# Moving the filter's second transform ahead of the first pair's ticks, with grouped turning transfers and another order at the borders

## The chip, the cores and the metric

The kernel runs on one core of one Trainium2 chip. The metric is device time in microseconds of a whole launch; lower is better. Engines are called PE (TensorE), DVE (VectorE), ACT (ScalarE), POOL (GpSimd) and SP (SyncE); PE writes to PSUM, eight banks of 512 f32 per partition, and DVE and ACT empty PSUM into SBUF.

## What is computed

A causal long convolution along the sequence, by FFT, and a spectral mixing layer behind it. Sizes: batch 8, sequence 5696, width 128, 64 modes.

```python
Xf = rfft(x, n=2*S, axis=1);  Hf = rfft(h, n=2*S, axis=0)      # x: (8, 5696, 128), h: (5696, 128)
x = irfft(Xf * Hf[None], n=2*S, axis=1)[:, :S, :]
X = rfft(x, axis=1)                                            # 64 modes are mixed
Yr = einsum('bmd,mde->bme', Xr, w_r) - einsum('bmd,mde->bme', Xi, w_i)
Yi = einsum('bmd,mde->bme', Xr, w_i) + einsum('bmd,mde->bme', Xi, w_r)
u = x + irfft(Y, n=S, axis=1)
out = u + maximum(u @ w_ch, 0)
```

## The kernel before

The sequence of 5696 is 89 rows of 64, and a transform of length 2 × 5696 is done in two steps. The **first transform** multiplies by F (the tile F1, 90 frequencies as 180 real columns). It is `a_tile(j)` for the input: 32 tiles of 4 matmuls with 180 columns each, into two PSUM banks, emptied by ACT or DVE into As (128x720). The **second transform** multiplies by the matrix M (`second`), four of the 90 frequencies at a time; such a group is a **tick**, and there are NT = 23 (the last has two frequencies). The input is worked in four pairs of batches (`g_` = 0 to 3).

In tick t of a pair PE and the other engines do four things, staggered so that they overlap: `second` (As and M into PSUM), `products` (ACT copies PSUM to Xs, DVE multiplies Xs by the filter Hs into U; L600), then with a lag of LC = 2 ticks the **third step** (U times Wc, 4 matmuls with 512 columns, cast by ACT into Zs or Zt, and written to the DRAM scratch zscr by SP), and with a lag of LM = 3 ticks the **modes** (Zs times G, added up in bank 7 over the whole pair, copied to XT at the end). `x_load` and `x_place` bring the next pair's input during the ticks, on POOL's DMA queue and on DVE.

The filter h goes through the same two transforms once. Its first transform (into Ah) is done ahead of everything while the input x arrives. Its second is `filter_tick(t)`: 16 small matmuls of Ah with M, one evacuation to Hs (128x512), and two DMAs on SP's queue that write a **turned copy**, the upper and the lower 64 partitions exchanged, into the second half of Hs (46 transfers in all); after every second tick up to the 11th a piece of G is loaded over the used part of Ah. Six filter ticks stand among the first pair's 32 tiles. The other 17 stand in the first pair's own ticks, six ticks ahead (LH), in banks 2 and 3 with DVE as the evacuating engine.

The first pair's ticks therefore have an order of their own: one `second` per tick, in banks 0 and 1 as long as the filter uses 2 and 3, all products from Xs, six buffers of Zs at first. In the other pairs two seconds are issued together every other tick (`twin`), in two alternating pairs of banks, and every fourth product is read from PSUM directly (`straight`).

The **border** between two pairs is written out by hand in the table `border`: a_tiles 0 to 5 of the next pair are put at given places in ticks 22 to 25, where the third steps and modes of the last ticks are still to be done; tiles 6 to 31 follow, ACT and DVE taking turns in a fixed pattern. `share(n)` is the other way to choose the engine: it keeps a running total for ACT and DVE by assumed costs (670 and 815 ns for 720 columns, 480 and 600 for 512) and gives the work to the one that is done earlier. `keep(n, bank)` issues n filler matmuls that keep PE going while it waits.

After the fourth pair come the mixing of the modes and the stage that makes the output (`u_z`, `u_tile`, `o_tile`).

All instructions go through a recorder that derives the waits from the tokens that each instruction reads and writes; each engine runs its own list in the order of issue.

Of the kernel before, what the change touches and what calls it, by code (L numbers as in the profile page):

```python
# [123 lines left out]
def bass_long_conv_fft__then__afno_spectral_mix_kernel(nc, x, h, moe_w_r, moe_w_i, moe_w_ch, out):  # L124
    B, S, D = x.shape
    M = moe_w_r.shape[0]
    assert D == P and M == 64 and B == 8
    J = 64
# [4 lines left out]
    NP = B // 2  # L133
    KT = 4
# [94 lines left out]
    NU, NXS, NZ, NZX = 3, 2, 6, 10  # L229
    NZS = [NZ] + [NZX] * (NP - 2) + [8]  # L230
    NZL = NZS[-1]
# [222 lines left out]

    def filter_tick(t, banks, eng="vector"):
# [84 lines left out]

    LC, LM, LH = 2, 3, 6
    ZR = 96
    XBANKS = [bank(0), bank(1), bank(2), bank(3)]

    def with_h_at(g_, t):
        return g_ == 0 and t + LH < NT

# [55 lines left out]
    Z_OLD = [("ag", k) for k in range(NS, NS + 8 * (NZX - NZ))]  # L603
    XPLACE = [9, 10, 12, 15, 16, 18, 20, 22], [9, 10, 13, 14, 17, 18, 20, 22]

    def zroom(g_, s_):
        return (s_ - 2 * NZ) % NZX if g_ == 0 and s_ >= 2 * NZ else s_ % NZS[g_]

    def xtok(n):
        return [("xt", n, p_) for p_ in range(2)]  # L610

    def tick(g_, t):
        if g_ + 1 < NP:
            for i in range(2 * XC):
                if t == XPLACE[g_ > 0][i]:
                    x_place(i, x_st[i], xtok(i))
        with_h = with_h_at(g_, t)
        if t < NT:
            of_two = t > 0 and twin(g_, t - 1)
            if not of_two and not (g_ == 0 and t > LC):  # L620
                second(g_, t)
            products(g_, t, slot_of(g_, t))
            if twin(g_, t):
                second(g_, t + 1)
                if straight(g_, t):
                    copied(g_, t + 1, slot_of(g_, t + 1))
        drain = list(border[t]) if t in border and g_ + 1 < NP else []
        if drain and t >= NT:
            j, sl, e = drain.pop(0)
            a_tile(j, [sl], e)  # L630
        if g_ + 1 < NP and t % 2 == 0 and 0 < t <= 4 * XC:
            i = t // 2 - 1
            x_load(g_ + 1, i, x_st[i], xtok(i), [("u", t % NU)] + AST)
        if LC <= t < NT + LC:
            s_ = t - LC
            n = len(ticks[s_])
            i, zi = s_ % NU, zroom(g_, s_)
            zb = [turns("z", ZBANK) for b in range(2)]
            for b in range(2):
# [9 lines left out]
                [("zs", zi, 0), ("zs", zi, 1)], [("zd", g_, s_)])  # L649
            if drain and t >= NT:  # L650
                j, sl, e = drain.pop(0)
                a_tile(j, [sl], e)
        if g_ == 0 and LC <= t < NT - 1:
            second(g_, t + 1)
        if LM <= t < NT + LM:
            s_ = t - LM
            zi = zroom(g_, s_)
            for b in range(2):
                for i, k in sorted(enumerate(ticks[s_]), key=lambda q: (s_ > 0 or q[1] != 1, q)):
                    if k % 2:  # L660
                        o, off, n, sl = pv(MB, b * P, [[1, P]]), (k + 1) // 2 * P, P, (k + 1) // 2
                    else:
# [5 lines left out]
                       k == 1 and b == 0, k == NK - 1 and b == 1, [("g", sl // GP), ("zs", zi, b)], [bank(MB)])  # L668
        if drain and t < NT + LM - 1:
            j, sl, e = drain.pop(0)  # L670
            a_tile(j, [sl], e)
        if with_h:
            filter_tick(t + LH, [2, 3])

    SLOTS = [0, 2, 4, 6]
    for j in range(32):
        a_tile(j, [turns("s", SLOTS)], "both" if j == 31 else share(720))
        if j >= 11 and j % 3 == 2 and (j - 11) // 3 < LH:
            b_ = turns("s", SLOTS)
            filter_tick((j - 11) // 3, [b_, b_ + 1], share(512))  # L680
    keep(12, turns("s", SLOTS))
    for g_ in range(NP):
        for t in range(NT + LM):
            tick(g_, t)
            if g_ == 0 and t < 2:
                keep(8, 4)
            assert g_ + 1 < NP or not wp
            if g_ == NP - 1 and t in early:
                pace[:] = [("u", min(t, NT - 1) % NU)]
                early[t]()  # L690
        evac(bass.AP(xt, 2 * g_ * XTW + M, [[B * XTW, P], [XTW, 2], [1, P]]), pv(MB, 0, [[P, 2], [1, P]]),
             [bank(MB)], [("xt", g_)], 1.0 / 64, eng="scalar", after=[("ag", k) for k in range(NS + 2 * XN, NK)])
# [199 lines left out]
```

## Time and profile before

| | us |
|---|---|
| median of 3 runs | 386.07 (385.49 to 386.13) |
| the profiled execution | 385.34 |
| its span, first to last instruction | 383.2 |
| PE busy | 366.0 (96%) |
| DVE busy | 310.5 (81%) |
| ACT busy | 302.7 (79%) |
| POOL busy | 82.5 (22%) |

A line of the profile names the source line, the engine, the operation, and output and input tiles by the program's names without buffer numbers; "x16" is a count. All matmuls are recorded by one helper (L320), so they are told apart by tiles: F,Xin is the first transform of the input, Ah,M the filter's second transform, As,M the input's second, U,Wc the third step, G with Zs or Zt the modes, and F alone is filler. ACT's As is L310, DVE's As L314; DVE's Hs is the filter's evacuation (L312). Times in the timeline are microseconds from the start of the span. Matmuls overlap, so the step from one start to the next tells what a group takes. The granted clock of TensorE (PEclk) is 1.00 at full speed.

### The profile page before, as it was taken

The numbers are of one execution on the slowest core, as the hardware profiler recorded it, in microseconds if no ns is written. First come the engines' busy times: TensorE is split into PE (matmuls) and PEld (weight loads), VectorE is DVE, ScalarE is ACT, GpSimd is POOL, SyncE is SP. The second block draws the span as 40 slices with busy tenths as digits, with TensorE's granted clock in tenths as the row PEclk, the third lists the DMA queues.
The fourth block names the chain that finished last, engine by engine and source line by source line (L and its number), as shares of the span: only waits on it lengthen the run. The fifth ranks groups of instructions, "written<-read, shape, count | busy, mean of one in ns | idle before, by whom it ended". The sixth has DMA issues, their size and how long they took to land.

```text
span 383.2 us, 12588 instructions
## 1 busy us (share of the span) xinstructions
PE 366.0 (96%) x5392; PEld 283.7 (74%) x5392; DVE 310.5 (81%) x348; ACT 302.7 (79%) x488; POOL 82.5 (22%) x133
## 2 busy tenths in 40 slices
PE   7999899999989999989999999999999999999994
PEld 7998756666866666866667866668898988887873
DVE  6969888998888999998998888875447767776876
ACT  1359688898889997989997999995457676776785
POOL 8400022220552320733310411319200000000000
PEclk9999999999999999999999999997999999999999
DMA  7998469999699997999995859999999999999879
GB/s 149 194 283 339 138 125 291 273 244 261 96 138 210 226 249 220 101 133 204 263 257 164 87 167 370 334 327 388 402 402 398 414 405 406 412 405 378 359 279 356
DMA packets 86865, 103.94 MB, mean 271 GB/s; under 512 B 22638, under 2 KB 72430, under 8 KB 83330
## 3 DMA queue, kind: packets, MB, share of 16 engines
q1 hardware_dynamic: 62523, 67.73, 50.5%
q0 software_dynamic: 24288, 35.43, 44.1%
q8 instruction: 42, 0.69, 0.7%
q14 instruction: 12, 0.10, 0.1%
HBM read 70.61 MB, written 51.12 MB: 318 GB/s over the span
## 4 chain that ended last, share of the span: by engine, by line
PE 69%; ACT 10%; DMA 9%; DVE 6%; POOL 2%; issue 2%; SPq 0%; DVEq 0%; POOLq 0%
PE ps L320 69%; ACT As L310 6%; DMA Xr<-in_x_dram 4%; DMA ZT0b<-zscr 4%; POOL Xr L317 2%; DVE As L314 2%; DVE U L592 1%; ACT UT L308 1%; ACT R L826 1%; ACT Zt L308 1%; DVE Xin L356 1%; ACT Xs L308 1%; DVE U L600 1%; DVE O L827 1%; DVE UT L312 0%
## 5 line engine op out<-in xcount | busy, mean ns | idle before, releaser
L600 DVE TENSOR_TENSOR U<-Xs,Hs 128x2048 f16<-128x2048 f16 (+1 forms) x73 | 86.7, 1190 | 12.0 <-ACT Xs L308 10.4
L320 PE MATMUL ps<-U,Wc 128*128 128x512 f16 (+1 forms) x368 | 94.0, 376 | 0.0
L308 ACT CAST Xs<-ps 128x1024 f16<-128x1024 f32 (+1 forms) x77 | 75.0, 979 | 9.0 <-PE ps L320 7.4
L308 ACT CAST Zs<-ps 128x512 f16<-128x512 f32 (+1 forms) x134 | 70.6, 596 | 5.9 <-PE ps L320 5.8
L827 DVE TENSOR_TENSOR O<-ps,R 128x512 f32<-128x512 f32 x81 | 52.6, 686 | 20.5 <-ACT R L826 15.2
L826 ACT ACTIVATE R<-ps 128x512 f32<-128x512 f32 x96 | 51.0, 573 | 14.2 <-PE ps L320 13.7
L314 DVE TENSOR_SCALAR As<-ps 128x720 f16<-128x720 f32 (+1 forms) x64 | 53.2, 880 | 5.1 <-PE ps L320 3.4
L320 PE MATMUL ps<-F,Xin 128*128 128x180 f16 x512 | 52.3, 250 | 2.6 <-DVE Xin L356 1.2
L320 PE MATMUL ps<-As,M 64*128 64x128 f16 x1440 | 50.6, 217 | 4.2 <-DVE U L592 3.0
L320 PEld LDWEIGHTS ps<-As,M 64*128 64x128 f16 x1440 | 40.3, 94 | 17.9 <-issue 8.1
L310 ACT ACTIVATE As<-ps 128x720 f16<-128x720 f32 x68 | 48.0, 768 | 6.4 <-PE ps L320 5.6
L320 PE MATMUL ps<-WI,UT 128*128 128x256 f16 x360 | 52.0, 279 | 0.5 <-DVE O L827 0.4
L320 PEld LDWEIGHTS ps<-F,Xin 128*128 128x128 f16 x512 | 44.5, 155 | 9.5 <-DVE As L314 2.6
L320 PEld LDWEIGHTS ps<-U,Wc 128*128 128x128 f16 x368 | 28.7, 97 | 27.6 <-ACT Zs L308 4.4
L317 POOL DMA_DIRECT2D Xt<-in_x_dram x48 | 26.0, 545 | 104.6 <-PE ps L320 100.2
L308 ACT CAST UT<-ps 128x712 f16<-128x712 f32 x40 | 30.0, 752 | 18.8 <-PE ps L320 17.8
L320 PEld LDWEIGHTS ps<-WI,UT 128*128 128x128 f16 x360 | 39.3, 152 | 4.4 <-issue 2.1
L320 PE MATMUL ps<-IBs,C 128*128 128x356 f16 x128 | 40.1, 323 | 0.6
L320 PEld LDWEIGHTS ps<-G,Zs 128*128 128x128 f16 x524 | 27.4, 96 | 11.7
L600 DVE TENSOR_TENSOR U<-ps,Hs 128x2048 f16<-128x2048 f32 x15 | 34.3, 2284 | 0.0
L320 PE MATMUL ps<-G,Zs 128*128 128x128 f16 (+2 forms) x524 | 32.6, 192 | 0.0
L320 PE MATMUL ps<-F 128*128 128x180 f16 x280 | 27.7, 254 | 2.5 <-DMA F<-cF 2.5
(86 smaller groups left out, 506.1 us busy)
## 6 DMA issues: line engine op xcount, KB each, us to landing
out_dram<-O SPq DMA_DIRECT2D x39, 512.0 KB, 11.4
zscr<-Zs SPq DMA_DIRECT2D x64, 256.0 KB, 6.8
Xt<-in_x_dram POOLq DMA_DIRECT2D x24, 320.0 KB, 7.0
zscr<-Zt SPq DMA_DIRECT2D x24, 256.0 KB, 6.6
W<-wscr POOLq DMA_DIRECT2D x4, 1024.0 KB, 8.9
M<-cM POOLq DMA_DIRECT2D x5, 720.0 KB, 20.5
ZT0a<-zscr SPq DMA_DIRECT2D x3, 1024.0 KB, 14.0
Hs<-Hs SPq DMA_DIRECT2D x44, 64.0 KB, 5.8
```

The costliest lines, as they stand in the source:

```text
L308: R.add(e, lambda h_: h_.copy(dst, src), reads, writes, after=after)
L310: R.add(e, lambda h_: h_.activation(dst, src, COPY, scale=scale), reads, writes, after=after)
L314: R.add(e, lambda h_: h_.tensor_scalar_mul(dst, src, scale), reads, writes, after=after)
L317: R.add(eng, lambda h_: h_.dma_start(dst, src), reads, writes, ring=ring, after=after)
L320: R.add("tensor", lambda h_: h_.matmul(o, l, r, start=st, stop=sp), reads, writes)
L356: R.add("vector", lambda e: e.tensor_copy(bass.AP(x_sb, i * XN * XS, [[XW, NQ], [XS, XN], [1, D]]), bass.AP(src, 0, [[XB, NQ], [D, XN], [1 ...
L592: R.add("vector", lambda e, b=b, s_=s_: e.tensor_tensor(bass.AP(u_s[i], b * 512, [[2048, P], [1024, 2], [1, n * D]]), s_, hv, MULT), [tok, ...
L600: R.add("vector", lambda e: e.tensor_tensor(uv, src, hv, MULT), bk + [("h", t, 0), ("h", t, 1, 0), ("h", t, 1, J)], [("u", i)])
L826: R.add("scalar", lambda e: e.activation(rv, src_r, RELU), bk, [("r", i % NR)], after=once(("r", i % NR), G_ALL + XTT + [("y", 0), ("y", 1 ...
L827: R.add("vector", lambda e: e.tensor_tensor(ov, src_u, rv, ADD), bk + [("r", i % NR)], [key + (h_,)], after=once(key, old))
```

## The change

All 23 filter ticks are done among the first pair's 32 tiles, in twos, spread out by `due`; share() chooses the engine for each. The turned copy is written in five groups of ticks (0 to 1, 2 to 5, 6 to 11, 12 to 17, 18 to 22), two transfers each. The first pair's ticks get the order of the other pairs, and the functions that made the difference are gone. The ticks of a pair with a successor end at 22; the third steps and modes that remain are written out with a_tiles 0 to 4 between them, and the engine of each tile at the border is chosen by share().

```diff
-    NZS = [NZ] + [NZX] * (NP - 2) + [8]
+    NZS = [NZX] * (NP - 1) + [8]
...
+    HEND = [1, 5, 11, 17, NT - 1]
...
     def filter_tick(t, banks, eng):
...
-        for p0, p1 in ((0, J), (J, 0)):
-            dma("sync", h_sb[p0:p0 + J, HW + lo:HW + hi], h_sb[p1:p1 + J, lo:hi], "s", [("h", t, 0)], [("h", t, 1, p0)])
+        if t in HEND:
+            g0 = ([-1] + HEND)[HEND.index(t)] + 1
+            lo = KT * g0 * D
+            for p0, p1 in ((0, J), (J, 0)):
+                dma("sync", h_sb[p0:p0 + J, HW + lo:HW + hi], h_sb[p1:p1 + J, lo:hi], "s", [("h", i, 0) for i in range(g0, t + 1)],
+                    [("h", i, 1, p0) for i in range(g0, t + 1)])
...
-    border = {NT - 1: [(0, 0, V)], NT: [(1, 2, V), (2, 0, V)], NT + 1: [(3, 2, A), (4, 0, V)], NT + 2: [(5, 2, V)]}
...
     def twin(g_, t):
-        return g_ > 0 and t % 2 == 1
+        return t % 2 == 1
     def straight(g_, t):
-        return g_ > 0 and t % 4 == 3
+        return t % 4 == 3
     def slot_of(g_, t):
-        if g_ == 0 or t == 0:
-            return XSLOT[(t + 1) % 2 if t and not with_h_at(g_, t) else 0]
+        if t == 0:
+            return XSLOT[0]
         return XSLOT[((t - 1) // 4 + t) % 2]
...
-    XPLACE = [9, 10, 12, 15, 16, 18, 20, 22], [9, 10, 13, 14, 17, 18, 20, 22]
+    XPLACE = [9, 10, 13, 14, 17, 18, 20, 22]
...
+    def tick(g_, t):
...
+        third(g_, t - LC)
+        modes_of(g_, t - LM)
...
     for j in range(32):
         a_tile(j, [turns("s", SLOTS)], "both" if j == 31 else share(720))
-        if j >= 11 and j % 3 == 2 and (j - 11) // 3 < LH:
+        due = NT if j == 30 else max(0, j - 2) * NT // 28 // 2 * 2
+        while done < due:
             b_ = turns("s", SLOTS)
-            filter_tick((j - 11) // 3, [b_, b_ + 1], share(512))
-    keep(12, turns("s", SLOTS))
+            filter_tick(done, [b_, b_ + 1], share(512))
+            done += 1
+    keep(8, turns("s", SLOTS))
     for g_ in range(NP):
-        for t in range(NT + LM):
+        for t in range(NT + LM if g_ + 1 == NP else NT):
             tick(g_, t)
-            if g_ == 0 and t < 2:
-                keep(8, 4)
...
+        if g_ + 1 < NP:
+            load.update(scalar=600.0, vector=0.0)
+            third(g_, NT - 2)
+            a_tile(0, [0], share(720))
+            a_tile(1, [2], share(720))
+            third(g_, NT - 1)
+            load["scalar"] += 560.0
+            a_tile(2, [0], share(720))
+            modes_of(g_, NT - 3)
+            a_tile(3, [4], share(720))
+            modes_of(g_, NT - 2)
+            a_tile(4, [2], share(720))
+            modes_of(g_, NT - 1)
+            load["scalar"] += 700.0
...
-            for j in range(6, 32):
-                a_tile(j, [(4, 6, 0, 2)[(j - 7) % 4] if j > 6 else 0], "both" if j == 31 else (A, V)[(j - 6) % 9 % 2])
+            for j in range(5, 32):
+                a_tile(j, [(0, 4, 6, 2)[(j - 5) % 4]], "both" if j == 31 else share(720))
                 if j == 31:
-                    keep(8, 6)
+                    keep(8, 2)
```

`third` and `modes_of` are the third step and the modes, taken out of `tick` unchanged.

More of the change, by code (lines that the diff above doesn't have):

```diff
@@ L539, in keep @@
             mm(pv(b0 + i % 2, 0, [[1, 2 * NK]]), f1_sb[:, 0:P], f1_sb[:, :], True, True, [("f1",)], [bank(b0 + i % 2)])
-    LC, LM, LH = 2, 3, 6
+    LC, LM = 2, 3
     ZR = 96
     XBANKS = [bank(0), bank(1), bank(2), bank(3)]
-    def with_h_at(g_, t):
-        return g_ == 0 and t + LH < NT
     onchip = {}
@@ L603, in bass_long_conv_fft__then__afno_spectral_mix_kernel, with third @@
     Z_OLD = [("ag", k) for k in range(NS, NS + 8 * (NZX - NZ))]
-    XPLACE = [9, 10, 12, 15, 16, 18, 20, 22], [9, 10, 13, 14, 17, 18, 20, 22]
+    XPLACE = [9, 10, 13, 14, 17, 18, 20, 22]
     def zroom(g_, s_):
-        return (s_ - 2 * NZ) % NZX if g_ == 0 and s_ >= 2 * NZ else s_ % NZS[g_]
+        return s_ % NZS[g_]
     def xtok(n):
         return [("xt", n, p_) for p_ in range(2)]
[L612 to L635, printed above, removed]
+    def third(g_, s_):
+        if 0 <= s_ < NT:
             n = len(ticks[s_])
@@ L649, in tick, with modes_of @@
                 [("zs", zi, 0), ("zs", zi, 1)], [("zd", g_, s_)])
[L650 to L656, printed above, removed]
+    def modes_of(g_, s_):
+        if 0 <= s_ < NT:
             zi = zroom(g_, s_)
@@ L668, in tick @@
                        k == 1 and b == 0, k == NK - 1 and b == 1, [("g", sl // GP), ("zs", zi, b)], [bank(MB)])
[L669 to L673, printed above, removed]
+    def tick(g_, t):
+        if g_ + 1 < NP:
+            for i in range(2 * XC):
+                if t == XPLACE[i]:
+                    x_place(i, x_st[i], xtok(i))
+        if t < NT:
+            of_two = t > 0 and twin(g_, t - 1)
+            if not of_two:
+                second(g_, t)
+            products(g_, t, slot_of(g_, t))
+            if twin(g_, t):
+                second(g_, t + 1)
+                if straight(g_, t):
+                    copied(g_, t + 1, slot_of(g_, t + 1))
+        if g_ + 1 < NP and t % 2 == 0 and 0 < t <= 4 * XC:
+            i = t // 2 - 1
+            x_load(g_ + 1, i, x_st[i], xtok(i), [("u", t % NU)] + AST)
+        third(g_, t - LC)
+        modes_of(g_, t - LM)
     SLOTS = [0, 2, 4, 6]
+    done = 0
     for j in range(32):
         a_tile(j, [turns("s", SLOTS)], "both" if j == 31 else share(720))
-        if j >= 11 and j % 3 == 2 and (j - 11) // 3 < LH:
+        due = NT if j == 30 else max(0, j - 2) * NT // 28 // 2 * 2
+        while done < due:
             b_ = turns("s", SLOTS)
-            filter_tick((j - 11) // 3, [b_, b_ + 1], share(512))
-    keep(12, turns("s", SLOTS))
+            filter_tick(done, [b_, b_ + 1], share(512))
+            done += 1
+    keep(8, turns("s", SLOTS))
     for g_ in range(NP):
-        for t in range(NT + LM):
+        for t in range(NT + LM if g_ + 1 == NP else NT):
             tick(g_, t)
-            if g_ == 0 and t < 2:
-                keep(8, 4)
             assert g_ + 1 < NP or not wp
```

3 lines of the change are left out of this document (2 added, 1 removed).

## The prediction

> **What bounds the kernel now.** I read the page first, for the engine shares and the chain that ended last, and then the table of stages cut at the places where TensorE (PE) goes from one kind of matmul to the next.
>
> ```profile
> span 383.2 us, 12588 instructions
> PE ps L320 69%; ACT As L310 6%; DMA Xr<-in_x_dram 4%; DMA ZT0b<-zscr 4%; POOL Xr L317 2%; DVE As L314 2%; DVE U L592 1%; ACT UT L308 1%; ACT R L826 1%; ACT Zt L308 1%; DVE Xin L356 1%; ACT Xs L308 1%; DVE U L600 1%; DVE O L827 1%; DVE UT L312 0%
> ...
> core 0: us, PE busy (x) PEld busy (x) DVE busy (x) ACT busy (x) POOL busy (x), PEclk, DMA share, GB/s
> 27.97:43.88 15.91, 15.76 (x236) 13.77 (x237) 14.58 (x19) 14.54 (x20) 0.00 (x0) 1.00 0.78 284
> 43.88:93.03 49.15, 48.00 (x884) 29.60 (x885) 41.87 (x49) 42.09 (x65) 8.89 (x16) 1.00 0.94 228
> 93.03:109.12 16.09, 15.34 (x165) 13.11 (x166) 14.61 (x18) 13.80 (x23) 8.51 (x12) 1.00 0.87 126
> 109.12:148.18 39.06, 37.77 (x605) 24.64 (x605) 36.38 (x32) 37.41 (x60) 9.40 (x18) 1.00 1.07 220
> 148.18:164.28 16.10, 15.33 (x164) 13.09 (x165) 14.60 (x18) 13.40 (x23) 7.77 (x11) 1.00 0.89 129
> 164.28:202.97 38.69, 37.47 (x604) 24.61 (x605) 36.38 (x32) 37.05 (x60) 10.52 (x19) 1.00 1.07 221
> ```
>
> The chain runs on PE for 69% of the span. The rows after it are, in order: the first pair's first transform (a_tile) with six filter ticks, the first pair's ticks, a border, the second pair's ticks, a border, the third pair's ticks. Each row gives length, then busy time by engine. Ticks and the stage before them keep PE nearly full: 48.00 of 49.15, 37.77 of 39.06. A border gives PE 15.33 of 16.10 but also DVE 14.60 and ACT 13.40, so it has two limits close together. The first pair's ticks last 49.15 us, the second's 39.06 and the third's 38.69 for the same transforms; the difference is the filter. The timeline of PE shows it inside one tick, first of pair one (with the filter, then late ones without), then of pair two:
>
> ```profile
> 58.59 0.62 PE L320 MATMUL ps<-As,M 64*128 64x128 f16 x16
> 59.14 0.50 PE L320 MATMUL ps<-G,Zs 128*128 128x2 f16 x8
> 59.57 0.41 PE L320 MATMUL ps<-Ah,M 64*128 64x64 f16 x16
> 59.91 1.04 PE L320 MATMUL ps<-U,Wc 128*128 128x512 f16 x4
> 60.88 0.62 PE L320 MATMUL ps<-As,M 64*128 64x128 f16 x16
> ...
> 85.55 0.62 PE L320 MATMUL ps<-As,M 64*128 64x128 f16 x16
> ...
> 87.39 0.62 PE L320 MATMUL ps<-As,M 64*128 64x128 f16 x16
> ...
> 126.59 1.07 PE L320 MATMUL ps<-As,M 64*128 64x128 f16 x32
> ...
> 130.12 1.07 PE L320 MATMUL ps<-As,M 64*128 64x128 f16 x32
> ```
>
> Columns are start and duration; I subtract starts, because the durations overlap. A tick of pair one takes 60.88 − 58.59 = 2.29 us with a filter tick in it and 87.39 − 85.55 = 1.84 without one; in pair two, two ticks take 130.12 − 126.59 = 3.53, or 1.76 each. In both, PE goes straight from one step to the next, so what is taken out of a tick shortens it.
>
> **The first pair's ticks.** The change takes 17 of the 23 filter ticks out of them, with 34 turning DMAs on SP's queue and 17 evacuations on DVE, as well as 16 filler matmuls, and runs them in the order of pairs two and three (twin ticks, every fourth product read from PSUM, ten z buffers). That order is measured: 39.06 and 38.69. I take 38.9, so this stage gives 49.15 − 38.9 = **−10.25 us** (bounds −10.1 and −10.5).
>
> **The first transform's stage.** The 17 ticks (the last has half the columns, so 16.5) land here, on PE as well as on the two engines that empty PSUM.
>
> ```profile
> 27.97 4.83 PE L320 MATMUL ps<-F,Xin 128*128 128x180 f16 x48 [0.48 <-DVE Xin L356]
> 32.73 0.41 PE L320 MATMUL ps<-Ah,M 64*128 64x64 f16 x16
> 33.07 1.16 PE L320 MATMUL ps<-F,Xin 128*128 128x180 f16 x12
> ...
> 40.67 1.97 PE L320 MATMUL ps<-F,Xin 128*128 128x180 f16 x20
> 42.63 1.10 PE L320 MATMUL ps<-F 128*128 128x180 f16 x12
> 43.88 0.62 PE L320 MATMUL ps<-As,M 64*128 64x128 f16 x16
> ...
> L310 ACT ACTIVATE As<-ps 128x720 f16<-128x720 f32 x19 | 14.1, 783 | 3.3 <-PE ps L320 3.1
> L314 DVE TENSOR_SCALAR As<-ps 128x720 f16<-128x720 f32 x12 | 10.5, 904 | 1.3 <-PE ps L320 0.9
> L312 DVE CAST Hs<-ps 128x512 f16<-128x512 f32 x6 | 4.1, 683 | 0.0
> L308 ACT CAST Zs<-ps 128x512 f16<-128x512 f32 x26 | 14.0, 610 | 0.0
> ```
>
> The first 12 tiles take 32.73 − 27.97 = 4.76 us, 0.397 a tile. A filter tick holds PE for 33.07 − 32.73 = 0.34 us. From 32.73 to 42.63 there are 20 tiles and 6 ticks: 9.90 − 20 × 0.397 = 1.96, or 0.33 a tick with whatever waits it causes. So 16.5 × 0.34 = 5.6 us are added.
>
> That price is only right if the evacuations keep up. Busy time over count gives 14.1/19 = 0.74 us a tile on ACT and 10.5/12 = 0.875 on DVE; both together finish a tile every 0.40 us. A filter tick is 0.683 on DVE; ACT has none here, and its nearest row, the cast of the same 128x512 from the second pair's ticks, gives 14.0/26 = 0.54; together one every 0.30. The new stage is 32 tiles and 22.5 ticks: PE 32 × 0.397 + 22.5 × 0.34 = 20.4 us; evacuation 32 × 0.40 + 22.5 × 0.30 = 19.6. PE stays ahead as the limit by 0.8 us, provided that share() divides the work evenly, which it does by a running total. All evacuations of pair one's ticks were on DVE; here ACT takes part, and that is what covers them.
>
> Filler shrinks from 12 matmuls to 8, but the second transform starts at 43.88, 1.25 us after the last tile's matmuls ended, on the last evacuation, so it only covers that wait. I give 0.2 us back: **+5.4 us**. Bounds: +4.6 if the slack in evacuation also removes most of the 1.25 us; +11.1 if each tick costs the full 0.683 on a saturated DVE (16.5 × 0.67). I stay near the lower, because the six ticks already there, all on DVE, cost 0.33.
>
> [...]
>
> **Waits that move.** The later ticks now need the matrix M early. The rows are its last two pieces, the sizes of a turned copy and of a load of G, and what the DMA engines moved (last column, GB/s) while M came in:
>
> ```profile
> L317 POOL DMA_DIRECT2D M<-cM x2: 552/554/555, 12.8 to 13.3; - x2
> DMA to landing us min/median/max: 23.0/24.4/25.7
> ...
> Hs<-Hs SPq DMA_DIRECT2D x44, 64.0 KB, 5.8
> G<-cG SPq DMA_DIRECT2D x5, 256.0 KB, 3.7
> ...
> 29.00:31.00 2.00, 2.00 (x22) 1.71 (x21) 2.00 (x3) 2.00 (x4) 0.00 (x0) 1.00 1.02 423
> ```
>
> The very last lands at 13.3 + 25.7 = 39.0. Tick 18 is the first that needs it, after 25 tiles and 18 ticks: 27.97 + 9.9 + 6.1 = 44.0. So there are 5 us to spare, and no wait. The turned copies, 10 transfers in place of 46, wait on SP for the last tick of their group, with G's loads queued behind them; the first pair's products need them from 49 us on, when the groups of ticks 0 to 17 have been issued, and the last group only some 30 us later. They cost nothing on the path, before as after: none of the 46 stands in the chain that ended last.
>
> **Borders, three of them.** The new order puts the third step of tick 21 ahead of a_tile 0, and lets share() place the evacuations.
>
> ```profile
> 147.31 0.49 PE L320 MATMUL ps<-G,Zt 128*128 128x4 f16 x8
> 148.18 0.85 PE L320 MATMUL ps<-F,Xin 128*128 128x180 f16 x8 [0.38 <-DVE Xin L356]
> 149.50 1.07 ACT L308 CAST Zs<-ps 128x512 f16<-128x512 f32 x2 [1.24 <-PE ps L320]
> 152.77 0.55 ACT L310 ACTIVATE XT<-ps 128x256 f16<-128x256 f32 x2 [0.35 <-PE ps L320]
> 154.29 9.05 PE L320 MATMUL ps<-F,Xin 128*128 128x180 f16 x92 [0.25 <-ACT As L310]
> 154.87 9.15 DVE L314 TENSOR_SCALAR As<-ps 128x720 f16<-128x720 f32 x11 [0.19 <-PE ps L320]
> 155.18 9.04 ACT L310 ACTIVATE As<-ps 128x720 f16<-128x720 f32 x13 [0.27 <-PE ps L320]
> ```
>
> Removed are PE's 0.38 us wait for Xin and ACT's 1.24 us without work. Going through the new order by hand with these durations, I get new waits in their place: tile 2 for its bank pair (0.3), tile 3 for the casts of tick 22 (0.2), tile 7 for the two XT copies out of bank 7 (0.5, by the 0.55 of their row). Tile 9 then starts within 0.1 us of the 154.29 above. From there PE (92 matmuls in 9.05), DVE and ACT are full alike, and an even division can save a few tenths. I take −0.25 each, **−0.75 us**; bounds −0.77 each (all of the 16.10 − 15.33 that PE idles there) and +0.3 each if the new waits aren't covered. The rest of the kernel is not touched and moves earlier as a whole. POOL gets 14 weight copies a border instead of 13, which nobody waits for.
>
> **The sum.** +5.4 − 10.25 − 0.75 = −5.6 us. The profiled execution took 385.34 us (span 383.2), so it would be 379.7. That execution lies 0.73 below the median of the runs, 386.07; applied to the median: **380.5 us**.
>
> **The rivals.** *Evacuation sets the first stage.* With PSUM slots waiting for DVE or ACT, a tick costs 0.48 to 0.5 instead of 0.34: +8 us there, gain 3, 383.1. For it: DVE and ACT were already busy 14.58 and 14.54 of 15.91. Against it: the ticks' casts are shorter per PE time than the tiles'. Were it the full 0.683, +11.1 would meet −11.0 and nothing would be gained. *Pair one does not reach the pace of pair two*, for instance 1.84 a tick, what pair one shows above without a filter; 23 × 0.08 = 1.8 us are lost, 382.3. Against it: the same code is measured twice. *The borders get worse* by 0.3 each: 382.2. *Slower: filter tick 18 waits for M.* G's loads and the turned copies now share the DMA engines with M. From 44.0 us every microsecond counts; slower than before it becomes once M lands later than about 44.0 + 5.6 + 0.8 = 50.4. G (6 loads of about 256 KB, 1.5 MB) and the copies of ticks 0 to 11 (12 × 128 KB, 1.5 MB), all ahead of M at the 423 GB/s of the row above, delay it by 7 us to 46, some 2 us of loss: 382.5. It takes a rate half as high, 53, to lose 9 us: 389.5. Against it: most of these transfers are issued after M has landed.
>
> **How the numbers follow.** Forecast 0.74 (377.9 to 383.4: its terms' bounds are 4.6 − 10.5 − 2.3 = −8.2 and, with a tick at 0.40 in the first stage, 6.5 − 10.1 + 0.9 = −2.7); evacuation 0.09, of which 0.02 no change and 0.02 slower; slower pace 0.07; borders 0.04; M 0.06, all of it in the severe form and so slower. About 0.2%, 0.77 us, is what a measurement of this kernel can tell from no change. Faster 0.90, same 0.02, slower 0.08. The range is the forecast's own, 378.0 to 383.4; it takes in the pace and border cases and the milder half of evacuation, and leaves out the M case and a tenth of what is left.
>
> **What would show it.** First second-transform matmul (As,M) near 49.3 us, between 48.5 and 50.4; first border tile 38.9 us later, near 88.2; then three borders of 15.5 to 16.1. In the first stage ACT should have about half of the Hs casts and PE no wait over 0.5 us. It is wrong if PE waits for M or for evacuation by more than 2 us there, if pair one's ticks take over 40 us, or if a border exceeds 16.4.

## The result, and the profile after

| | before | after |
|---|---|---|
| median of 7 runs each, us | 385.77 (384.55 to 386.13) | 383.67 (382.61 to 384.32) |
| the profiled execution, us | 385.34 | 384.32 |
| its span, us | 383.2 | 382.2 |

The change makes the kernel faster by 2.1 us: ratio 0.9941 [0.992, 0.9961]. The forecast was 5.6 us. The profiled execution of after happens to be the slowest of its seven, so its span shows only 1.0 us of the gain. Most of what is missing was lost in the first stage, at one place, and the cause is not one of the prediction's rivals: PE had no instructions to execute.

First the profile page of after, then its table of stages, cut as before at PE's changes from one kind of matmul to the next (length, then busy time and count by engine, granted clock, share of the DMA engines, GB/s).

```profile
span 382.2 us, 12483 instructions
PE 362.2 (95%) x5372; PEld 284.0 (74%) x5372; DVE 307.4 (80%) x334; ACT 304.0 (80%) x497; POOL 81.9 (21%) x133
PEclk9999899999999999999999999998999999999998
```

```profile
core 0: us, PE busy (x) PEld busy (x) DVE busy (x) ACT busy (x) POOL busy (x), PEclk, DMA share, GB/s
27.88:53.60 25.72, 22.65 (x497) 19.33 (x497) 19.46 (x25) 19.41 (x31) 0.00 (x0) 0.93 0.96 282
53.60:92.73 39.13, 38.28 (x609) 24.95 (x610) 36.85 (x32) 37.50 (x61) 8.30 (x16) 1.00 0.97 221
92.73:108.12 15.39, 14.58 (x163) 12.72 (x161) 13.33 (x17) 13.81 (x23) 9.24 (x13) 1.00 0.99 136
108.12:147.26 39.14, 38.27 (x609) 24.94 (x609) 36.83 (x32) 37.50 (x61) 9.39 (x18) 1.00 1.07 223
147.26:162.52 15.26, 14.54 (x161) 12.65 (x160) 13.34 (x17) 13.80 (x23) 8.75 (x12) 1.00 0.97 131
...
216.93:382.20 165.27, 155.72 (x2280) 126.62 (x2280) 115.98 (x149) 120.99 (x204) 19.87 (x24) 0.98 0.95 360
```

Read the clock column first. The stages of ticks and borders run at 1.00; the first transform's has 0.93, and there PE is busy for 22.65 of 25.72 us where the neighbouring rows are nearly full. The PEclk line of the page shows the same as the 8 in its fifth slice; the dip in slice 28, most of what gives the last row its 0.98, is in before too. Against the table of before:

| stage | before | after | difference | forecast |
|---|---|---|---|---|
| up to the first tile | 27.97 | 27.88 | −0.09 | 0 |
| first transform, filter ticks | 15.91 | 25.72 | **+9.81** | +5.4 |
| pair one's ticks and border | 65.24 | 54.52 | −10.72 | −10.5 |
| pair two's ticks and border | 55.16 | 54.40 | −0.76 | −0.25 |
| pair three's ticks and border | 54.78 | 54.41 | −0.37 | −0.25 |
| the rest | 164.14 | 165.27 | +1.13 | 0 |
| sum | 383.2 | 382.2 | −1.0 | −5.6 |

The timeline of PE in the first stage shows the hole:

```profile
40.42 0.78 PE L320 MATMUL ps<-Ah,M 64*128 64x64 f16 x32
41.19 0.70 PE L320 MATMUL ps<-F,Xin 128*128 128x180 f16 x6
44.46 0.32 PE L320 MATMUL ps<-F,Xin 128*128 128x180 f16 x2 [2.58 <-issue]
44.71 0.64 PE L320 MATMUL ps<-Ah,M 64*128 64x64 f16 x32
45.28 1.43 PE L320 MATMUL ps<-F,Xin 128*128 128x180 f16 x8
```

The wait of 2.58 us falls into the middle of two a_tiles, between the sixth and the seventh of eight matmuls of one kind, and its releaser is "issue": no semaphore, no other engine and no data that the profile shows. What came after is the second loss. Eight matmuls take 1.43 us at 45.28, but 0.85 us at 49.98 in the same timeline: the clock was granted at half, 0.5 for 3.41 us from 45.36 on in the trace's record of it.

The stretches of 2 us around it, in the columns of the table of stages:

```profile
39.00:41.00 2.00, 2.00 (x66) 1.73 (x60) 1.65 (x3) 2.00 (x4) 0.00 (x0) 1.00 1.03 279
41.00:43.00 2.00, 0.88 (x21) 0.70 (x13) 1.64 (x3) 0.88 (x2) 0.00 (x0) 1.00 1.06 247
43.00:45.00 2.00, 0.54 (x22) 0.44 (x23) 0.00 (x0) 0.18 (x1) 0.00 (x0) 1.00 1.02 223
45.00:47.00 2.00, 2.00 (x47) 1.68 (x40) 1.54 (x2) 1.31 (x3) 0.00 (x0) 0.59 0.94 230
47.00:49.00 2.00, 2.00 (x37) 1.91 (x32) 0.75 (x2) 1.62 (x3) 0.00 (x0) 0.56 0.61 159
```

DVE and ACT are not the limit (0.00 and 0.18 busy in the worst slice, they have nothing to evacuate), while the DMA engines are full at 1.02 to 1.06 (the time of the packets that begin in a stretch, as a share of 16 engines, so it can pass 1). The one DMA queue that I take to concern PE, and that stands for no tile, is in the page's list of queues (packets, MB, share); the second fence is that list for the 0.1 us from 41.6 to 41.7:

```profile
q8 instruction: 42, 0.69, 0.7%
```

```profile
q1 hardware_dynamic: 9, 0.02, 119.8%
q8 instruction: 1, 0.02, 81.2%
```

42 packets and 0.69 MB are 16.4 KB each, and the trace holds 5372 matmuls and as many weight loads, 10,744 records: about 256 PE instructions for a packet. I read from this that queue 8 brings PE its program; the run fewer_fill below bears it out. The fourth packet starts at 41.64 us and ends at 42.94, and PE, which had stopped at 41.88, goes on at 44.46. PE runs out when a single block is late, some 190 instructions behind the point at which that block comes in the run hold below. In before no wait of PE over 0.15 us in this stage ends by "issue"; in after one of 2.58 us does.

Beside it, SP's own queue (start, time of the issuing instructions, tile, count) shows what the change had put there by then:

```profile
31.75 1.18 SPq L317 DMA_DIRECT2D Hs<-Hs  x2
32.97 1.40 SPq L317 DMA_DIRECT2D G<-cG  x2
35.31 1.11 SPq L317 DMA_DIRECT2D Hs<-Hs  x2
36.46 2.05 SPq L317 DMA_DIRECT2D G<-cG  x3
```

The turned copies and G's loads were spread from 34 to 86 us before. Now two of the five groups and five of the six G loads are handed over by 38.5 us, and the third group from 40.15 on, while M is still coming in on POOL's queue.

### The profile page after: what moved, and what is told of

It reads as the page before. It is cut to its first block, busy times and chain, and to the rows that moved or that the text cites. A ratio compares the mean times of both kernels' runs of the same rounds, so it can differ in the third digit from the quotient of the medians.

```text
span 382.2 us, 12483 instructions
## 1 busy us (share of the span) xinstructions
PE 362.2 (95%) x5372; PEld 284.0 (74%) x5372; DVE 307.4 (80%) x334; ACT 304.0 (80%) x497; POOL 81.9 (21%) x133
## 4 chain that ended last, share of the span: by engine, by line
PE 78%; ACT 9%; DMA 5%; DVE 5%; issue 2%; SPq 0%; DVEq 0%
PE ps L320 78%; ACT As L310 7%; DMA ZT0b<-zscr 5%; DVE As L314 2%; DVE U L594 1%; ACT R L832 1%; ACT UT L308 1%; DVE O L833 1%; DMA F<-cF 0%; DVE UT L312 0%; ACT XT L310 0%; SPq L317 0%; PE ps L786 0%; DVE Os L833 0%; DVEq L105 0%
## 5 line engine op out<-in xcount | busy, mean ns | idle before, releaser
L602 DVE TENSOR_TENSOR U<-Xs,Hs 128x2048 f16<-128x2048 f16 (+1 forms) x68 | 80.6, 1188 | 10.7 <-ACT Xs L308 9.6
L308 ACT CAST Xs<-ps 128x1024 f16<-128x1024 f32 (+1 forms) x72 | 69.5, 971 | 7.0 <-PE ps L320 4.8
L308 ACT CAST Zs<-ps 128x512 f16<-128x512 f32 (+1 forms) x126 | 66.1, 605 | 0.0
L832 ACT ACTIVATE R<-ps 128x512 f32<-128x512 f32 x96 | 51.0, 573 | 16.0 <-PE ps L320 15.5
L314 DVE TENSOR_SCALAR As<-ps 128x720 f16<-128x720 f32 x64 | 53.5, 880 | 8.5 <-PE ps L320 7.2
L320 PE MATMUL ps<-F,Xin 128*128 128x180 f16 x512 | 54.6, 253 | 4.3 <-issue 2.6
L310 ACT ACTIVATE As<-ps 128x720 f16<-128x720 f32 (+1 forms) x68 | 49.0, 773 | 11.9 <-PE ps L320 10.7
L320 PE MATMUL ps<-As,M 64*128 64x128 f16 x1440 | 48.6, 217 | 4.5 <-DVE U L594 3.5
L602 DVE TENSOR_TENSOR U<-ps,Hs 128x2048 f16<-128x2048 f32 x20 | 45.7, 2284 | 0.0
L308 ACT CAST Zt<-ps 128x512 f16<-128x512 f32 (+1 forms) x58 | 31.0, 605 | 0.0
L320 PE MATMUL ps<-G,Zs 128*128 128x2 f16 (+2 forms) x492 | 30.3, 191 | 0.0
```

What stands on the lines that cost most here:

```text
L308: R.add(e, lambda h_: h_.copy(dst, src), reads, writes, after=after)
L310: R.add(e, lambda h_: h_.activation(dst, src, COPY, scale=scale), reads, writes, after=after)
L314: R.add(e, lambda h_: h_.tensor_scalar_mul(dst, src, scale), reads, writes, after=after)
L320: R.add("tensor", lambda h_: h_.matmul(o, l, r, start=st, stop=sp), reads, writes)
L602: R.add("vector", lambda e: e.tensor_tensor(uv, src, hv, MULT), bk + [("h", t, 0), ("h", t, 1, 0), ("h", t, 1, J)], [("u", i)])
L832: R.add("scalar", lambda e: e.activation(rv, src_r, RELU), bk, [("r", i % NR)], after=once(("r", i % NR), G_ALL + XTT + [("y", 0), ("y", 1 ...
```

## The experiments

**Theories.** That PE waited for instructions was a reading of the trace; *why the fetch was late* was open. Either it stood behind data in the DMA engines (of G; of the copies with their long pieces; of M), or PE simply consumed 256 instructions faster than they can come, whatever the DMA engines do. Where an expectation uses letters, A is the bytes of G's loads and of the copies, A2 the bytes of M, which the others delay, B an accident of one execution, C and E the long pieces, D the pace of PE alone, F bytes and their pace whatever the length of the pieces.

The table below is read from single packets of queue 8 and from PE's records (these are not rows of a view). "Beside M" is what SP had issued by 37.7 us: sizes and counts from the list of DMA issues.

| kernel | beside M, KB | fourth fetch, us | PE records before it | PE's wait, us | first stage, us |
|---|---|---|---|---|---|
| after | 1792 | 41.64 to 42.94 | 1215 | 2.58 | 25.72 |
| after_again | as after | 42.16 to 43.41 | 1217 | 2.87 | 26.90 |
| g_late | 1024 | 41.50 to 42.76 | 1207 | 2.10 | 25.13 |
| both_late | 1280 | 41.80 to 43.13 | 1213 | 2.54 | 25.60 |
| turn_1k | 1280 | 41.79 to 42.94 | 1217 | 2.66 | 25.60 |
| turn_46 | 768 | 39.48 to 40.46 | 1106 | none | 21.86 |
| hold | 0 | 37.71 to 38.99 | 1025 | none | 21.86 |
| hold_g_late | 0 | from 37.71 | 1029 | none | 21.88 |
| hold_oldborder | 0 | from 37.46 | 1021 | none | 21.84 |
| hold_pad | 1440, behind M on POOL | 40.03 to 40.96 | 1135 | 0.45 | 22.29 |

PE has the same pace in all of them up to its wait: from the first tile to filter tick 12 it takes 12.52 to 12.56 us. Where nothing is beside M, the fourth fetch comes at 37.5 to 37.7 us and 1021 to 1029 records; I take that as when a fetch comes here if nothing holds it back. (When it is asked for can't be seen; in before it begins at 958 records.) PE stops at about 1217 records, 4.0 us later. That is not all slack: in the six rows with a wait PE goes on 1.4 to 1.6 us after the end of the fetch, 2.3 to 2.9 us after its beginning. So PE stalls in the six rows whose fetch ends at 40.96 or later, and in the four whose fetch ends by 40.46 (the two not given end by 38.6) it does not.

**after_again**: the changed kernel, unedited.

> The changed kernel once more, as the measure for the other three. In its first profile PE stood idle for 2.58 us at 41.88 us, with nothing in the profile that released it, and its clock then was granted at half for 3.41 us. Theory A (PE runs out of instructions, because the fetch of its next block waits on DMA engines that are full of G loads and turned copies) expects the idle of 2 to 3 us again near the same place, the first stage at 25 to 26 us, and 383 to 384 us. Theory B (a single accident of one execution) expects no such idle, the first stage at about 21.5 us and a time that is at most 1 us from the 383.7 measured before, the loss then lying elsewhere.

Measured: median 384.12, ratio 0.9949 [0.9923, 0.9974]. The hole is there again, 2.87 us, with 6.83 us at half clock behind it instead of 3.41. It belongs to the kernel and not to one execution.

**g_late**: all but the first of G's loads moved out of the filter's ticks into pair one's.

```diff
-        if t % 2 and t // 2 < NG:
-            ... dma("sync", g_sb[...], ...)
+        if t == 1:
+            load_g(0)
...
+            if g_ == 0 and t % 4 == 0 and t // 4 + 1 < NG:
+                load_g(t // 4 + 1)
             tick(g_, t)
```

> Five of the six G loads (1.2 MB) are moved from the first transform's stage into the first pair's ticks 0, 4, 8, 12 and 16; the turned copies stay as they are in the change. Theory A: there is less for the DMA engines at 33 to 44 us, PE's idle shrinks to under 1 us or is gone, the clock stays at 1.00, the first stage takes 21.5 to 23.5 us, and the time is 379.5 to 382. Theory C (the fetch waits because the turned copies have long descriptors of 2 to 6 KB, not because of the bytes) expects the idle to stay at 2 us or more and 383 to 384. Theory D (PE simply uses up instructions faster than they can be fetched when so many filter ticks stand there, whatever DMA does) expects the same, 383 to 384.

Measured: 383.51, ratio 0.9926 [0.9896, 0.9956]; a wait of 2.10 us stays. G's 768 KB less moved the fetch by 0.1 to 0.7 us only. That G's bytes are the cause falls, at least as the whole of it.

**both_late**: G as in g_late, and the last three groups of turned copies issued ahead of ticks 0, 5 and 10 of pair one.

```diff
-        if t in HEND:
+        if t in HEND[:2]:
+            turned(t)
...
+            if g_ == 0 and t in (0, 5, 10):
+                turned(HEND[2 + t // 5])
```

> As the one before, and the turned copies of ticks 6 to 11, 12 to 17 and 18 to 22 are issued at ticks 0, 5 and 10 of the first pair, so that only M, one G load and 0.77 MB of turned copies are left in the first transform's stage. Theory A: no idle over 0.5 us, clock 1.00, the first stage at 21 to 22 us, 379 to 380.5. Theory C: the same or nearly. Theory D: idle of 2 to 3 us as before, 383 to 384. If the product of tick 6 waits for its turned copy, the first pair's ticks are over 40 us.

Measured: 391.33, ratio 1.0141 [1.0098, 1.0184], and the hole is as before. It did not test what it should: SP had nothing ahead of the third group, and issued it at 40.45 us all the same. What it lost elsewhere is on PE's timeline, in the modes of pair one:

```profile
90.87 0.56 PE L320 MATMUL ps<-G,Zs 128*128 128x128 f16 x5 [4.02 <-DMA G<-cG]
```

G's last piece was issued at 89.63, behind writes to zscr on SP's queue. Moving loads late enough to be harmless at 38 us made them late at 87; pair one's ticks took 47.56 us.

**turn_46**: after with the turned copy in 46 transfers again.

```diff
-    HEND = [1, 5, 11, 17, NT - 1]
+    HEND = list(range(NT))
```

> The turned copy is written in 46 transfers of one tick each again (1 KB descriptors), issued right after each filter tick; all else as in the change. SP issues one in some 0.55 us, so that the same bytes are spread from 31 to 60 us. Theory A: fewer bytes wait at 41 us, the idle is under 1 us, 379.5 to 382. Theory C: idle gone as well, 379 to 381. Theory D: idle stays, 383 to 384.

Measured: 387.02, ratio 1.0013 [0.9982, 1.0044]: no gain that can be measured. The profile has no hole and 21.86 us in the first stage, so it speaks against the pace of PE alone as the cause. But pair one's ticks take 44.05 instead of 39.13. The reason is on the queue of SP (first row) and on ACT (second):

```profile
53.36 15.97 SPq L317 DMA_DIRECT2D Hs<-Hs  x22
...
73.72 1.07 ACT L308 CAST Zs<-ps 128x512 f16<-128x512 f32 x2 [3.04 <-DMA zscr<-Zs]
```

SP issues 22 copies in 15.97 us, 0.73 each, and until 69.4 us pair one's writes of Zs wait behind them; then ACT has no Zs buffer. So the grouping in the change is needed, and what it costs is paid elsewhere. (The profiled execution took 384.36 us, 2.66 less than the median; what the others lose besides isn't in it and stays open.)

**hold**: after, with every turned copy made to wait for the last piece of M as well. G's loads stand behind them on SP.

```diff
-  "s", [("h", i, 0) for i in range(g0, t + 1)],
+  "s", [("h", i, 0) for i in range(g0, t + 1)] + [("m", MP - 1)],
```

> The change with one more wait: the turned copies, and with them the G loads behind them on SP's queue, are not issued before M's last piece has landed. Number and size of the transfers and PE's order stay. In the five runs so far the fetch of PE's fourth block of instructions began between 0.1 us before and 1.4 us after the last piece of M had landed (38.6 us in the kernel before, 39.6 with 46 transfers, 40.6 to 41.4 in the others), and PE had used up its instructions at 41.7. Theory A2 (that fetch stands behind M on one DMA engine, and the copies and G loads that share this engine push M's end from 38.6 to 41) expects M's end at 38 to 39, the fetch by 40, no idle over 0.5 us, clock 1.00 in the first stage, the stage at 21.5 to 22.5 us, and 379 to 380.5. Theory C (the length of the copies' descriptors matters, wherever they stand) expects a stall of 2 to 3 us, perhaps later, and 383 to 384.

Measured: **379.72** (before beside it 385.75), ratio 0.9845 [0.9819, 0.9871]. This is the fastest version, ahead of both kernels. Its first three rows are the first stage, pair one's ticks and the second border; the last is a stretch in which after has its fetch pending:

```profile
28.03:49.89 21.86, 21.23 (x496) 18.05 (x497) 19.26 (x25) 19.18 (x31) 0.00 (x0) 1.00 0.80 270
49.89:89.41 39.52, 38.45 (x608) 24.95 (x609) 36.76 (x32) 37.53 (x61) 8.30 (x16) 1.00 1.06 251
143.92:159.20 15.28, 14.55 (x163) 12.65 (x161) 13.34 (x17) 13.81 (x23) 8.75 (x12) 1.00 1.01 139
...
37.00:39.00 2.00, 2.00 (x55) 1.66 (x55) 1.83 (x3) 1.77 (x4) 0.00 (x0) 1.00 0.08 23
```

M has landed at 38.3 us here, 41.1 in after. The DMA engines are at 0.08 when the fetch begins, where after has over 1.0, PE never stops, and the clock stays at 1.00. The first stage is 3.86 us shorter than after's: 2.58 of the wait, and 1.28 for the rest, which fits 3.41 us at half clock (1.7 at most).

**hold_pad**: hold, with two more pieces of 720 KB each, read into space that is free then and used by nothing, behind M on POOL's queue.

```diff
+    for i in range(2):
+        dma("gpsimd", pad_sb[i][:, :], bass.AP(c_m, i * 2880, [[MW, P], [1, 2880]]), "x", ...)
```

> As the one before, with 1.4 MB of M read a second time into unused space, behind M on the same queue and needed by nobody. Theory A2: the fetch now stands behind these bytes; they end near 42 us, PE runs out of instructions at 41.7 again, with an idle of 1 to 3 us, and the time is 1 to 4 us above the run without them. Theory C: nothing changes against the run without them, within 0.7 us.

Measured: 380.27, ratio 0.9859 [0.9828, 0.989]. Other data alone makes the fetch late, by 2.3 us, without copies and without G, and PE's timeline has a short wait (this kernel's lines are numbered one higher):

```profile
41.17 0.70 PE L321 MATMUL ps<-F,Xin 128*128 128x180 f16 x6
42.33 0.32 PE L321 MATMUL ps<-F,Xin 128*128 128x180 f16 x2 [0.45 <-issue]
```

It stands between the same two matmuls as the wait of after, at the same 1217 records, 1.37 us behind the end of the fetch. The stage is 0.43 us longer than hold's, at a clock of 1.00. So data on the DMA engines is enough for a wait, though for less than the 1 to 3 us that were expected; the medians differ by 0.55 us, with overlapping intervals. The fetch begins at 40.03 while the last of the extra data lands at 42.53, so it does not stand behind every byte that was issued before it.

**hold_oldborder**: hold with the table `border`, the fixed pattern of engines and the bank of the eight fillers as before the change.

```diff
-            for j in range(5, 32):
-                a_tile(j, [(0, 4, 6, 2)[(j - 5) % 4]], "both" if j == 31 else share(720))
+            for j in range(6, 32):
+                a_tile(j, [(4, 6, 0, 2)[(j - 7) % 4] if j > 6 else 0], "both" if j == 31 else (A, V)[(j - 6) % 9 % 2])
...
```

> As the first of this set, but with the borders in the order and with the division between ACT and DVE of the kernel before. By the two traces a pair with its border takes 55.16 and 54.78 us before and 54.40 and 54.41 after, so the border's new order is worth 0.4 to 0.8 us each: 1.2 to 2.3 us longer than the first of this set. If the prediction's 0.25 each were right, 0.75.

Measured: 381.29, ratio 0.9899 [0.9868, 0.993]. The table of stages for its second pair and border:

```profile
104.54:143.23 38.69, 37.47 (x605) 24.60 (x605) 36.38 (x32) 37.05 (x60) 9.39 (x18) 1.00 1.08 219
143.23:159.32 16.09, 15.35 (x164) 13.10 (x164) 14.61 (x18) 13.75 (x23) 7.78 (x11) 1.00 0.92 137
```

A border is 16.09 us in the old order and 15.28 in the new one, but the new cut has 0.45 more in the ticks (a third step was moved ahead of a_tile 0). Together 54.78 against 54.42: 0.36 a border, and 1.57 between the medians. It shows in pairs two and three alone: pair one with its border takes 54.86 in this profile and 54.89 in hold's, whose ticks there are 0.4 longer than after's.

**before_again**: the kernel before, unedited, one execution.

> The kernel before once more, for its profile. From the fourth pair's first second-transform matmul to the end it took 164.14 us in its one profile, against 165.2 to 165.3 in four of the changed kernel and its variants and 163.7 in a fifth. If the last part is really shorter there, it comes out within 0.2 of 164.1 again; if it only scatters, anywhere from 163.7 to 165.3.

Measured: 385.26. Its stages agree with before's within 0.25 us up to the last part, which takes 163.83 there.

**turn_1k**: after, with the groups that end at ticks 5, 11 and 17 each written in pieces of 1 KB, even and odd ticks apart.

> The change, with the turned copies of ticks 2 to 5, 6 to 11 and 12 to 17 written in pieces of 1 KB instead of 4 and 6 KB: each group in four transfers (even and odd ticks apart) instead of two, at the same places in SP's queue and beside M. In the run that let the copies wait, the fetch began at 37.7 us with the DMA engines nearly idle; so it is asked for then, and 4.0 us later PE has used up what it has. With copies of 1 KB (46 transfers) it began 1.8 us late, with M alone 2.3, with long pieces beside M 3.8 to 4.5. Theory E (the fetch waits for its turn on one DMA engine, longer the longer the pieces of the other queues in front of it) expects the fetch at 40.5 at the latest, an idle under 1 us and 380 to 382. Theory F (only bytes and their pace count: the 46 transfers helped because SP issued them slowly) expects the fetch at 41.3 to 42, an idle of 2 to 3 us and 383 to 384.

```diff
+                if t in (5, 11, 17):
+                    for odd in range(2):
+                        w = [[2 * HW, J], [1024, (t + 1 - g0) // 2], [1, 512]]
+                        dma("sync", bass.AP(h_sb, p0 * 2 * HW + HW + lo + odd * 512, w), ...)
+                    continue
```

Measured: 383.33, ratio 0.9939 [0.9919, 0.996]; fetch at 41.79, wait 2.66 us. Long pieces are not the cause.

**hold_g_late**: hold and g_late together.

> The copies wait for M's last piece, and five of the six G loads are issued during the first pair's ticks. In the run with the waiting copies alone, the sixth fetch came some 2 us late and the first pair's ticks took 39.52 us instead of 39.12. Theory E: less stands beside the copies at 40 to 50 us, the ticks take 39.1 to 39.3, and the time is 0 to 0.5 us below that run: 379.2 to 379.8. Theory F expects the same. If a mode step waits for its G, the ticks are over 39.6 and the time above 380.

Measured: 380.61, ratio 0.987 [0.9847, 0.9893]. Pair one's ticks go to 39.12, 0.4 us less than hold's, but the median is not below hold's, and their intervals overlap. G's place is worth nothing measurable once the copies wait.

**before_long**: the kernel before, with the copies of ticks 0 and 1, and of 2 to 5, in groups as in after.

```diff
+        ends = [1, 5] + list(range(6, NT))
+        if t in ends: ...
```

> The kernel before, with the turned copies of its first six filter ticks in two groups (ticks 0 to 1 and 2 to 5, the sizes of the change). Its first stage uses PE's instructions more slowly: six filter ticks, not 23. Theory E: a fetch may begin later than the 36.1 and 39.9 us of the kernel before, but PE does not run out: no idle over 0.5 us with nothing that released it before 44 us, the first stage at 15.9 to 16.3 us, the time within 0.7 of the kernel before. If long pieces alone are enough for a stall, whatever PE's pace, the first stage is 1 us or more longer.

Measured: 385.58, ratio 1.0003 [0.9979, 1.0027]. No hole: the fourth fetch comes at 40.45 against 39.93 in before, at 989 and 958 records. Grouping alone costs nothing where fewer PE instructions are used up in the time.

**fewer_fill**: after, with 64 fewer warming matmuls at the start and 18 fewer after the filter's first transform, so that other instructions stand at the ends of the blocks.

```diff
-    WARM = 138
+    WARM = 74
...
-        for i in range(4 if j < 15 else 30):
+        for i in range(4 if j < 15 else 12):
```

> The change with 82 filler matmuls fewer ahead of the first stage (64 of the first 138 and 18 of the 30 just before the input's tiles); transfers and all else as in the change. 82 weight loads and 82 matmuls fewer move the point at which the next block of 256 instructions is asked for 164 instructions deeper into the first stage, at some 50 a microsecond about 3.3 us later: 41.0 us instead of 37.7, when M is done or nearly done, and the point at which PE would run out to about 45. If the idle belongs to the instruction count, it is no longer at 41.7 us; the fetch waits less, idle under 1 us, the first stage 21.9 to 23 us, and 380 to 381.5. If it belongs to the time or to the tile (a full DMA system at 41 to 44 us, the 22nd tile), it stays at 41 to 45 us with 2 to 3 us, and 383 to 384. Less filler may let PE's clock be granted at half while the filter's first transform begins; that would show as a later start of the first stage.

Measured: 390.62, ratio 1.0128 [1.0096, 1.016]. I had expected the hole to go; it did not. PE's timeline has a shorter one earlier, and the long one is still there, but at another tile:

```profile
36.52 0.77 PE L320 MATMUL ps<-F,Xin 128*128 128x180 f16 x7 [1.01 <-issue]
44.59 1.36 PE L320 MATMUL ps<-F,Xin 128*128 128x180 f16 x8 [2.78 <-issue]
53.52 0.57 PE L320 MATMUL ps<-F,Xin 128*128 128x180 f16 x4 [1.58 <-DVE As L314]
```

At the three waits PE has 705, 961 and some 1217 records behind it: 256 apart. Fetches of queue 8 begin at 34.16, 41.68 and 50.95, next to each. (The third is put down to DVE by the profile. But PE goes on 1.56 us after the end of that fetch, 51.96, and in the two others 1.30 and 1.67 us after the end of theirs.) The long wait begins at 41.8 us as in after, so by this one alone the time could be the cause; the two others begin at 35.5 and 51.9. The stops follow the count of instructions and not the tile, nor M, which had landed at 37.9. What fewer filler costs besides is clock: half speed for 6.83 us from 12.8 on, and again with the second wait and behind the third, 0.83 on average in the stage, which takes 30.58 us.

**What is shown and what is open.** Shown: PE stops because its next instructions have not come; the fetch comes late when data fills the DMA engines (at 41.64 us in after and 40.03 in hold_pad, against 37.71 in hold); keeping the copies and G's loads out of M's time removes the wait and brings the gain that was forecast. Open: what in the DMA engines holds the fetch back. It does not go by bytes alone (1024 KB beside M in g_late made it as late as 1792 KB in after, the pad's 1440 KB only 2.3 us), nor by the length of the pieces, and a packet's request cannot be seen in the trace, only its transfer. Open too: what fills the 1.3 to 1.7 us from the end of that transfer to PE's next matmul.

## Why the prediction was right or wrong

**The first stage, +5.4, was the step that failed: +9.81.** Its working on PE and the evacuations was right. Without the hole the stage takes 21.86 us (hold, turn_46), +5.95, within 0.6 of the forecast and inside the bounds. PE and not evacuation sets it: 21.23 of 21.86 busy, and ACT takes 14 of the 23 evacuations of Hs (7.7 us), DVE 9 (6.1), as counted on. The rival "evacuation sets the first stage" gave nearly the same number as was measured, 383.1, but for a reason that the trace excludes. The sum of the prediction's bounds took +6.5 as this term's worst, and not the +11.1 that it gives as the term's own bound; 9.81 lies between the two. No run shows the 0.40 us a tick from which that +6.5 comes: in hold the 22 full ticks take 0.28 to 0.38 us each, 0.35 on average. (The 0.34 us for a tick of 16 small matmuls is 21 ns each, an average: in before's first filter tick the starts come in pairs, 3 or 4 ns apart, a pair every 29 ns. The 0.34 us for the 16 holds.)

**"They cost nothing on the path" is the sentence at fault.** The turned copies and G were costed by when their data is used, and M by when it lands; both are right: M came 2.8 us later than in hold, at 41.1, and nobody waited for it. What the sum left out is that the DMA engines also carry PE's instructions, and that PE can wait for these: 2.58 us, and 1.28 more in the stage, which fits the half clock. The page of before lists queue 8 with its 42 packets, and the prediction did not ask what it carries and for whom. It had the shared engines in view in its rival on M, but priced M's landing alone, and set against it that "most of these transfers are issued after M has landed". That was wrong: in after 2.0 of the 3.0 MB counted there had been issued by 38.5 us, ahead of M's end at 41.1. The numbers for a warning were there: the new stage uses 256 instructions in about 5 us, where before's needed 8.1 between its fourth and fifth fetch (39.93 and 48.02), and the copies and loads were moved into the time in which M already fills the engines.

**Pair one's ticks, −10.25, and the borders, −0.75, were right in the main.** The pace of pairs two and three came out in pair one: 39.13, a gain of 10.02, just under the bound of 10.1. With the border 10.72 us were gained against 10.5 forecast. In pairs two and three a border gained 0.36 and 0.40 by hold against hold_oldborder, a little over the forecast 0.25, and at 15.26 to 15.39 they end just below the 15.5 that was given, because the new order moves a third step ahead of the cut.

**The signs that were named worked.** "As,M near 49.3" came at 53.60, and "It is wrong if PE waits for M or for evacuation by more than 2 us there" pointed at the place, though not at the kind of wait. In hold, As,M comes at 49.89 and the first border tile at 89.41 (88.2 forecast), and the gain is 6.0 us by the medians against 5.6 forecast. By its profile the stages ahead of the last part give 5.5, so the forecast was the price of the change without the wait for instructions. The M rival, the one on the slower side, did not occur.

**The rest of the kernel, +1.13, is not settled.** The change does not touch it. Over the profiles of these kernels, but for fewer_fill, it takes 163.7 to 165.3 us, 163.83 and 164.14 in the two of before, 164.7 in before_long, which has the same code there, and 164.2 in hold_g_late. In after the chain of waits shows a transfer that lasts longer than the same one of before (the first fence is the chain of after, the second that of before):

```profile
330.52 17.78 DMA ZT0b<-zscr
```

```profile
332.77 16.55 DMA ZT0b<-zscr
```

That is the size of the difference, but no run here varied it, and the same transfer takes 16.85 us in g_late, whose last part is as long (165.3). So the transfer alone does not explain it, and by the scatter it may be chance.

## What to carry to other kernels

In these runs PE's instructions come through the DMA engines, 16.4 KB or about 256 of them at a time, and other data alone made a fetch 2.3 us late (hold_pad). So the cost of a transfer that nobody waits for was not zero where PE runs through many small matmuls (2.58 us of wait in after's first stage): look at queue 8 (its number in these profiles) beside the DMA share, and take a wait of PE that ends by "issue" in the middle of one kind of matmul as a sign of it. When work is packed closer, ask of each transfer that moves with it not only when its data is needed but what else is on the engines then; a wait for a transfer that is already under way (here one more token, M's last) can be worth more than an early start: 379.72 us in hold against 383.67 in after. And the hole cost more than its length: of the waits for instructions in the first stage, those of 1.58 us and more had 3.4 or 6.8 us of half clock with them or behind them, and those of 0.45 and 1.01 us had none.

## What the hardware showed that was not expected

- PE stops dead for want of instructions when data holds up their fetch (in after with the DMA engines at 1.02 to 1.06): 2.1 to 2.9 us at this place in the profiles of after, after_again, g_late, both_late and turn_1k, 0.45 us in hold_pad, and none in the variants of after whose fourth fetch had ended by 40.46 us. A fetch lasts 0.9 to 1.4 us once it begins, and PE goes on 1.3 to 1.7 us after its end (42.94 and 44.46 in after).
- In this stage some 190 PE instructions, 4.0 us of work, lie between the point at which the fourth fetch begins in hold (1025 records) and the point at which PE is out (1217). With some 2.5 us from the beginning of a fetch to PE's next matmul, about 1.5 us of delay can go unnoticed, an estimate from these rows; hold_pad's 2.3 us already cost 0.45.
- Transfers of one size take longer in the crowd: in the list of issues a G load of 256 KB lands after 10.9 us in after, and after 3.7 in before.
